# A linear-attention block with a gated MLP: two PSUM banks, two engines' copies, one early load and a new issue order

## The chip, the cores and the metric

The kernel runs on one core of a Trainium2 chip. The metric is the device time of one execution in microseconds, as a median over several executions. A profile is one further execution with the hardware profiler on; its span is some 2 us shorter than the timed figure, so spans are compared with spans and medians with medians. All profiled runs here ran at a granted TensorE clock of 1.0 and are of state fast.

## The reference, cut to what matters

The input x has 2048 tokens of 512 features, all in bf16. The attention is linear: phi(q) and phi(k) in place of a softmax, 32 heads of 16 features.

```python
phi = lambda t: jnp.where(t > 0, t + 1, jnp.exp(t)) + 1e-06
pq, pk = (phi(q), phi(k))
kv  = jnp.einsum('bhsd,bhse->bhde', pk, v)
z   = jnp.einsum('bhsd->bhd', pk)
num = jnp.einsum('bhqd,bhde->bhqe', pq, kv)
den = jnp.einsum('bhqd,bhd->bhq', pq, z)[..., None] + 1e-06
o   = num / den
...
h  = x + o @ wo                               # after a layer norm of x in front
z  = gelu(layernorm(h) @ w_in)                # 2 x 896 features
z1, z2 = z[..., :896], layernorm(z[..., 896:])
g  = jnp.einsum('ts,bsf->btf', w_sp, z2) + b_sp[None, :, None]
h2 = h + (z1 * g) @ w_out
```

In the kernel, z1 is called the ungated half, z2 the gated half. The kernel folds kv and wo into one 512 x 512 matrix m, so that h is one product of pqT (phi of q, divided by the denominators) with m, plus x.

## The kernel before

The program first lists its operations, each with the tiles that it reads and writes, and from these works out every dependence. Then an issue order, a stored list of 1011 operation numbers, fixes in which order each engine issues its own. An operation waits by semaphore for what it depends on, so the order changes waits and never results. The parts that matter:

```python
ORDER = "c-jrogMtt..."                      # cut: 1011 operation numbers, packed
...
load_x("SP", 0, 1, 2150)                    # x0: one tile of 128 tokens, 128 KB
load_x("ACT", 1, 1, 2300)
x2 = load_x("SP", 2, 1, 2300)
load_x("ACT", 3, 1, 2550)
first_load("SP", wqkv[:, 0:2, D:2 * D], ..., "wka", 4200)       # K weights, 256 KB each
wk = first_load("ACT", wqkv[:, 2:4, D:2 * D], ..., "wkb", 4400)
for n, lat, behind in ((4, 3000, x2), (6, 3200, x2), (8, 3850, wk), ...):
    load_x("SP", n, 2, lat, behind)         # two tiles, 256 KB, held until `behind` has landed
```

```python
for c in range(KD):                          # m = kvm . wo, four column blocks
    b = CB[1 - c % 2]
    matmuls(bank(b), [(kvm[:, c, :], wo[:, c, :])])
    act(m[:, c, :], bank(b), ACT.Copy, GW)
```

The ungated half is made of six tile columns by Strassen's scheme, in cells of seven products of two matmuls each (0.43 us), and of a seventh column by plain, "classical", products of four matmuls (0.86 us). A cell owns the four banks 4 to 7, in one of two rotations. What counts is what must happen between the products of one cell:

```python
def strassen(k, q, banks, p5):
    A, B, C, E = banks
    ...
    matmuls(quad(A), list(zip(w11, a11)))
    copy(bank(B), bank(A))                                  # ScalarE
    matmuls(quad(E), list(zip(t1, s1)))
    copy(p5, bank(E))                                       # ScalarE
    matmuls(quad(A), list(zip(w21, a12)), **onto)
    gelu(k, q, 0, A)
    matmuls(quad(B), list(zip(t2, s2)), **onto)             # needs the first copy
    dve(... bank(C) = bank(B) + p5 ...)                     # line 856, VectorE
    matmuls(quad(B), list(zip(t3, s3)), **onto)             # writes the bank that line 856 reads
    ...
for q in (0, 1):
    for tg in (2 * q, 2 * q + 1):
        classic(KF - 1, tg, 6)                              # seventh column, bank 6
    ...
    for k in range(HF):
        strassen(k, q, ZB[cells % len(ZB)], p5z[cells % 2])
```

Because the classical products of the second half of the tokens use bank 6, and come first in program order, they must be done, GELU included, before a Strassen cell of that half writes bank 6.

The first products of the gates (each eight matmuls, 1.73 us) and the products of the gated half (also eight, in bank pairs 0/1 and 2/3) are independent of the cells. I call such a group a filler: it keeps TensorE streaming while another engine reads a bank.

Of the kernel before, what the change touches and what calls it, by code (L numbers as in the profile page):

```python
# [8 lines left out]
ACT = mybir.ActivationFunctionType  # L9
ALU = mybir.AluOpType  # L10

P = 128
# [3 lines left out]
ORDER = "c-jrogMttU00qE@tj)G<d$VoZwz=81ZQHhO+jiZ}FHA&4MpVQ_03sm@q9HnBASPlVHsT;Y5+E1yAUE;?AdJumgRlsO;0S?m2#=5uk{}V1A{mk+1yUju5+fh-BNYmu5YnPNDxw0Kpb{D(9uguo(x4y;BONlJ2+|`EnUE1hQ4Cp88C8%OjnNcYP!-uw1KCj=-BAKv(F5I364j6c)zJ*i(Go4t6TQ#}z0n3WQ46h53bj!Obx|5+Fb3mL5A`t?<FO1&upDjC8aYuG<<K7O&>sWP7yZxy4bTvSFc3@85uI=t2XO?4FaZ-W8I!OAE3q0=Fb#vT4na7IV~BuNIDz9Bg5el}kywLK7>%izj?U<U8JLOrSb&o_jagWT^;nBDIE5E@iOG73DVnP1c!t@SgP|CP4cLf9Sd2~Bf$f-!dDx6C*o!^biGA3G-8hG{*otj9kNr4+E4YelxPaukh!jexRJx8ExP+Uyj9Yk%*LZ_hxQ#owi~G2T2MErG2*HqihX{Ox07m3{JjN4*W>|({DE`DJe83NU#AkfLH^kt-|GR(TJHFx%Vlo!PGaP>-G9xi6qi~wyG7e)i9#b(IQ!_L3Fh8>}I`c9O$*eRBFdqvtEz>bQGcY5?zX--mEXA^{$%M?t?99QOEX`a@z;cYwKo(+Q7GY7=VKLTXU6$YyCSqciXBpP!V%B2|wq^xZWF=N+71n11He@3<W^N{7awcVQCS!NDWG}8^8&+ixR%Z(KW;3Q_6Sm?~F5_CZWlwJ5R+eOHZDShs;ZP3a6pr9jj^uRC;Bby&HP&ELHfMTeP&>9~U+!UMrBzn#Wfo;uPMu*oWm5-sWIuLdS7uUwX4G~L;AoEFSPo<^1u?hssWS(09LIA9cXB4DaTaHDIp=UL=kYAh@jTaY0w?hT^XLe3sDJ{MSA~>cg;iWdRZvBAhwHh4CA5(jSxP0<jnmbIGc<$~IiLGjM!UG1`+0yzSxm=xmz7jnl~qnxc$}Mfj|+K_D|mt{d6I*<fQvYpr+A4oHA}NKM{|`-^E6)zv`~vwR^@e-Z&*QZSy4}TjaBrN&sbH}^oRHPjt^K}?^#0+d7Xb*Tc=r9{|G(j3*O)(zT{0d)nhi+WxnET-r{E7CiQ_e^@Yt<OJDhobrfFTxrz}KponUsAN<LW{Kfiepcbm9;0mFTil_K$rr$io!%U#n3?<3>#Lx<(u!^SWilKyxsYFVwBx<NeYOS_vshw)2U23CtilktQtoHiMSW2o+imfP$qi~9<xZ0?#I<L;^pdRX~ZtAED>aL#ZqCM)PUh1oU8mMjRuT8q7!RoC68ls^Zra>C6AdS)p?bB&J)M%a2SdGzmZP5;$)plLc1dY@<P0~88)_QH$8g0;8?bjn+)NUQrL><*$9nxhT&@mm?RUOuK9nn*r&~2U5HGS7f-O(vM(Oo^$3%%AGJr{gKFZDw=^;oZTPm8rgOSMePwL&YkN^kW}A9YK$d|warUVrsdAM{0E^+})gOW*Wce^kY^9L#n~|5H5&cL;ZIeTQ@?hjBQEc0&g^g2OtzQ#+EYx|$<9s-ro&J359_Ii{<-iPN~YV>_1PxRc{Mq2s!<<2i{FyM_}uk<&VzlRKHyJEJqWsq470Gdq(TIE$M(tFt?&v$>UPI*)U^ky|^5bGe`cozHEY--TSnh270{-POfh)XiPoJzUCVT*4*Y$E97?E!@)O+{JBO(cN9%ecjHL+|TXZ)6+f3z1-WAJ;hT!%`-gHgFVZ$-QNQ|$8$Zz^SsdWy};|e!Hd1fOT5ur9pvF2=*>Rv6CUAB9_lUL=3yS`?cV7Ze(6yj>m45Lah~Au9^;9g<Xzt5WnSUkUgNbs<&!?`Gd}BA-sipE@1?%z<v!r^KIhk7<&{3_BR=GVzTn5c<jcO|Cw}Uye&%bw;ak4r>%QsRe&`3j=evIEcYf~=PT>Ns?1;|mbx!IEj^Z~y=EHvO)qdpr{^<VzBaZh("  # L16
# [236 lines left out]
def bass_sequential_preLN__linear_attn_block__mixer_gmlp__prompt_kernel(  # L253
# [241 lines left out]
    for n, lat, behind in ((4, 3000, x2), (6, 3200, x2), (8, 3850, wk), (10, 4000, wk), (12, 4200, wk), (14, 4400, wk)):  # L495
        load_x("SP", n, 2, lat, behind)
# [234 lines left out]
    for c in range(KD):  # L731
        b = CB[1 - c % 2]
        matmuls(bank(b), [(kvm[:, c, :], wo[:, c, :])])
        act(m[:, c, :], bank(b), ACT.Copy, GW)
# [5 lines left out]
    DB, MERGE = 6, ()  # L740
# [7 lines left out]
    for tg in range(NG):  # L748
# [12 lines left out]
        if tg not in MERGE:  # L761
# [3 lines left out]
            for t in range(first, tg + 1):  # L765
                for c in range(0, KD, 2):
                    q, r = pqT[:, c:c + 2, t * GW:(t + 1) * GW], r16[t // 2][:, c:c + 2, t % 2, :]
                    dve(lambda v, q=q, r=r: v.tensor_tensor(q, q, r, ALU.mult), [q, r], [q], 2 * GW, acc=2)
# [116 lines left out]
    cells = 0  # L885
    for q in (0, 1):
        a11, a12, a21, a22 = (hx[:, 2 * i:2 * i + 2, 4 * q:4 * q + 4, odd, :] for odd in (0, 1) for i in (0, 1))
        for tg in (2 * q, 2 * q + 1):
            classic(KF - 1, tg, 6)
            for fc in CLASSIC.get(tg, ()):  # L890
                classic(fc, tg, 6)
# [193 lines left out]
```

## Time and profile before

| | before |
|---|---|
| time, median of 3 runs | 230.85 us (230.7 to 230.99) |
| profiled span | 229.2 us |
| TensorE busy | 221.9 us, 97% |
| VectorE, ScalarE, GpSimd busy | 174.5, 109.6, 47.7 us |

The view that the argument rests on most is the chain of work that ended last, in order of time: start, length, engine, output tile, line. Wherever it leaves PE, TensorE waited. One place of it that the prediction does not show is between two products of the gated half (L807 and L810), right after ScalarE has loaded its GELU table:

```profile
69.30 0.86 PE psum L807 x4
70.16 0.65 PE psum L810 x4
70.81 0.02 issue
70.83 1.04 PE psum L807 x4
```

Two such products stand back to back, and the second takes 1.04 us where its like takes 0.86: it waits for ScalarE to empty a bank.

For small stalls I use the starts of the matmul records: the step from one start to the next, less the step that this width has in packed stretches (0.216 us for 512 columns). I call the sum over a stretch its lost time. Matmuls that start together (the four of a group of denominators, within 0.01 us of each other) count as no loss and no gain. In the first traces of before and after one record in 49 is missing (1168 of 1191 are there), and the doubled steps at those places (shown as 0.05 us "issue") are left out. Steps from one kind of matmul to another have fixed costs of up to 0.1 us that all kernels share.

### The profile page before, as it was taken

The page shows a single profiled execution, that of the slowest core. Times are in us where ns is not written, and L with a number is a line of the kernel's source. Part 1 is how long each engine was busy: PE and PEld are TensorE (multiplying, and loading weights), DVE is VectorE, ACT ScalarE, POOL GpSimd, SP SyncE. Part 2 cuts the span into 40 slices and gives each one's busy share as a digit, 9 for nine tenths or more (in the row PEclk, how much of TensorE's full clock was granted, in tenths as well). Part 3 has the DMA queues.
Part 4 walks back from the last instruction along what each step waited for, and adds up shares of the span by engine and source line. Part 5 has one row for each costly group of instructions (what it writes and reads, how often), then busy time and mean ns, then how long its engine had stood idle before and what let it go on. Part 6 is the DMA issues. An engine that isn't in the chain of part 4 may idle for free.

```text
span 229.2 us, 3241 instructions
## 1 busy us (share of the span) xinstructions
PE 221.9 (97%) x1168; PEld 110.0 (48%) x1191; DVE 174.5 (76%) x347; ACT 109.6 (48%) x205; POOL 47.7 (21%) x134
## 2 busy tenths in 40 slices
PE   8899999999899999999999999999999999999995
PEld 7344444453344444444434444444455555555553
DVE  3999756937996979489988888678738688885295
ACT  5695943499889989999456102100022122021110
POOL 3444400000764584467600000000000000000000
PEclk9999999999999999999999999999999999999999
DMA  6942469928645149499900799800000000020025
GB/s 186 280 131 47 93 177 331 268 79 196 147 108 106 38 92 111 96 184 224 125 0 1 153 234 177 172 0 0 3 0 0 0 26 24 0 69 3 0 83 169
DMA packets 58896, 23.68 MB, mean 103 GB/s; under 512 B 48512, under 2 KB 58752, under 8 KB 58880
## 3 DMA queue, kind: packets, MB, share of 16 engines
q1 hardware_dynamic: 58176, 22.88, 44.8%
q10 hardware_dynamic: 704, 0.59, 0.8%
q8 instruction: 9, 0.15, 0.2%
q14 instruction: 7, 0.06, 0.1%
HBM read 7.47 MB, written 2.10 MB: 42 GB/s over the span
## 4 chain that ended last, share of the span: by engine, by line
PE 91%; DVE 2%; issue 2%; POOL 1%; DMA 1%; ACT 1%
PE psum L402 72%; PE psum L807 6%; PE psum L659 6%; PE psum L810 5%; DMA x<-in_A_x_dram 1%; ACT sh L421 1%; DVE h L981 1%; DVE h L781 1%; POOL rs L550 1%; ACT m L421 0%; PE psum L755 0%; POOL st L534 0%; PE psum L680 0%; PE psum L569 0%; PE psum L724 0%
## 5 line engine op out<-in xcount | busy, mean ns | idle before, releaser
L421 ACT ACTIVATE psum<-psum 128x256 f32<-128x256 f32 (+1 forms) x39 | 17.7, 467 | 83.6 <-PE psum L402 57.0
L402 PE MATMUL psum<-wsp,z 128*128 128x512 bf16 x200 | 47.6, 379 | 0.4
L402 PEld LDWEIGHTS psum<-wsp,z 128*128 128x128 bf16 x208 | 20.4, 98 | 22.5 <-ACT psum L421 0.2
L421 ACT ACTIVATE e<-psum 128x1024 bf16<-128x1024 f32 (+1 forms) x18 | 16.7, 927 | 12.7 <-PE psum L402 12.0
L402 PE MATMUL psum<-t,s 128*128 128x512 bf16 x96 | 22.5, 379 | 0.0
L421 ACT ACTIVATE z1T<-psum 128x512 bf16<-128x512 f32 x28 | 16.1, 601 | 8.1 <-PE psum L402 5.5
L402 PE MATMUL psum<-wsp 128*128 128x256 bf16 (+1 forms) x89 | 19.3, 315 | 0.4 <-DVE psum L856 0.4
L402 PE MATMUL psum<-wout,z1T 128*128 128x256 bf16 (+1 forms) x82 | 16.5, 314 | 0.1
L807 PE MATMUL psum<-win,hnT 128*128 128x512 bf16 x63 | 16.2, 379 | 0.1
L989 DVE TENSOR_TENSOR u<-psum,bsp 128x512 bf16<-128x512 f32 x16 | 11.0, 689 | 6.0 <-PE psum L402 5.9
L402 PE MATMUL psum<-xnT,wqkv 128*128 128x512 bf16 x61 | 15.2, 379 | 0.2
L659 PE MATMUL psum<-pk,xn 128*128 128x512 bf16 x64 | 15.3, 379 | 0.0
L421 ACT ACTIVATE z<-psum 128x896 bf16<-128x896 f32 x16 | 14.6, 913 | 1.3 <-PE psum L810 1.0
L402 PE MATMUL psum<-wqkv,xnT 128*128 128x512 bf16 x61 | 14.7, 379 | 0.2
L402 PE MATMUL psum<-m,pqT 128*128 128x512 bf16 x62 | 14.4, 379 | 0.3 <-DVE h L781 0.2
L989 DVE TENSOR_TENSOR u<-psum,p 128x512 bf16<-128x512 f32 x12 | 8.3, 688 | 8.1 <-PE psum L402 8.0
L402 PEld LDWEIGHTS psum<-t,s 128*128 128x128 bf16 x96 | 9.4, 98 | 10.0
L810 PE MATMUL psum<-win,hnT 128*128 128x384 bf16 x64 | 13.0, 326 | 0.0
L510 DVE BATCH_NORM_STATS2 st<-x 128x6 f32<-128x512 bf16 x15 | 9.7, 677 | 3.8 <-DMA x<-in_A_x_dram 3.8
L781 DVE SCALAR_TENSOR_TENSOR h<-psum,x 128x512 bf16<-128x512 f32 x16 | 10.8, 686 | 2.1 <-PE psum L402 2.1
L534 POOL TENSOR_SCALAR st<-st 128x1 f32<-128x1 f32 x10 | 3.9, 391 | 40.0 <-ACT sh L421 32.2
L402 PEld LDWEIGHTS psum<-wsp 128*128 128x128 bf16 x90 | 8.2, 98 | 8.2 <-DVE psum L856 1.0
(125 smaller groups left out, 382.4 us busy)
## 6 DMA issues: line engine op xcount, KB each, us to landing
r<-rcp SPq DMA_DIRECT2D x16, 128.0 KB, 2.7
out_dram<-h SPq DMA_DIRECT2D x15, 128.0 KB, 1.7
win<-in_B_w_in_dram SPq DMA_DIRECT2D x2, 896.0 KB, 5.5
x<-in_A_x_dram SPq DMA_DIRECT2D x6, 256.0 KB, 4.2
wqkv<-in_A_wqkv_dram SPq DMA_DIRECT2D x2, 512.0 KB, 5.8
wout<-in_B_w_out_dram SPq DMA_DIRECT2D x1, 896.0 KB, 7.3
wo<-in_A_wo_dram SPq DMA_DIRECT2D x1, 512.0 KB, 6.7
bsp<-in_B_b_sp_dram SPq DMA_DIRECT2D x1, 512.0 KB, 4.9
```

Source lines behind the costliest of these rows:

```text
L402: inst = pe.matmul(out_ap, lhsT=a, rhs=b, start=start and i == 0, stop=stop and i == len(pairs) - 1, **kw)
L421: return g.add("ACT", lambda ac: ac.activation(out_ap, in_ap, func, **kw), [in_ap, *extra], [out_ap] + ([accum] if accum is not None else []),
L510: dve(lambda v: v.bn_stats(s[:, 0:6], src[:, n, :]), [src[:, n, :]], [s[:, 0:6]], D)
L534: pool(lambda p: p.tensor_scalar(s[:, 2:3], s[:, 0:1], s[:, 0:1], -1.0 / (n * n), op0=ALU.mult, op1=ALU.mult), [s[:, 0:1]], [s[:, 2:3]], 240)
L550: pool(lambda p: p.tensor_tensor(r, ve, expo[:, 0:1], ALU.pow), [ve, expo], [r], 620)
L659: inst = pe.matmul(bank(CB[c]), lhsT=xn[:, i, c * P:(c + 1) * P], rhs=pk[:, i, :], start=i == 0, stop=i == NT - 1)
L781: dve(lambda v, n=n, b=b, s=s: v.scalar_tensor_tensor(h[:, n, :], bank(b), 1.0, x[:, n, :], op0=ALU.mult, op1=ALU.add, accum_out=s[:, 0:1] ...
L807: pe.matmul(bank(b), lhsT=hnT[:, c, n * P:(n + 1) * P], rhs=win2[:, c, 0:GW], start=c == 0, stop=c == KD - 1)
L810: inst = pe.matmul(bank(b + 1, F2), lhsT=hnT[:, c, n * P:(n + 1) * P], rhs=win2[:, c, GW:FH], start=c == 0, stop=c == KD - 1)
L981: dve(lambda v, o=o, q=q, add=add: v.tensor_tensor(o, q, add, ALU.add), [q, add], [o], DH2, ps=True)
L989: dve(lambda v: v.tensor_tensor(t, bank(b), add, ALU.add), [bank(b), add], [t], GW, ps=True)
```

## The change

The intent: give the last classical products banks that the pairs of the gated half have left, so that their place is less bound; halve ScalarE's copies of m; have x4 and x5 at hand earlier. The issue order was made anew for this.

```diff
-ORDER = "c-jrogMttU00qE@tj)G<d$VoZwz=81ZQ..."      (cut)
+ORDER = "c-jTQ17HvU00h8Cwq47%ZQHhO+qGre..."        (cut)
@@
-    for n, lat, behind in ((4, 3000, x2), (6, 3200, x2), (8, 3850, wk), ...
+    for n, lat, behind in ((4, 4600, None), (6, 3400, x2), (8, 3850, wk), ...
@@
         matmuls(bank(b), [(kvm[:, c, :], wo[:, c, :])])
-        act(m[:, c, :], bank(b), ACT.Copy, GW)
+        if c % 2:
+            dve(lambda v, c=c, b=b: v.tensor_copy(m[:, c, :], bank(b)), [bank(b)], [m[:, c, :]], GW, ps=True)
+        else:
+            act(m[:, c, :], bank(b), ACT.Copy, GW)
@@
+    last = [next_pair() + i for i in (0, 1)]           # banks 0 and 3
     for q in (0, 1):
         for tg in (2 * q, 2 * q + 1):
-            classic(KF - 1, tg, 6)
+            classic(KF - 1, tg, last[tg - 2] if q else 6)
```

The rest of the diff is a switch (PM) that would put products of pqT on GpSimd. It is empty in the change, so it does nothing there.

More of the change, by code (lines that the diff above doesn't have):

```diff
@@ L15 @@
 SEM_NS = 45.0
-ORDER = "c-jrogMttU00qE@tj)G<d$VoZwz=81ZQHhO+jiZ}FHA&4MpVQ_03sm@q9HnBASPlVHsT;Y5+E1yAUE;?AdJumgRlsO;0S?m2#=5uk{}V1A{mk+1yUju5+fh-BNYmu5YnPNDxw0Kpb{D(9uguo(x4y;BONlJ2+|`EnUE1hQ4Cp88C8%OjnNcYP!-uw1KCj=-BAKv(F5I364j6c)zJ*i(Go4t6TQ#}z0n3WQ46h53bj!Obx|5+Fb3mL5A`t?<FO1&upDjC8aYuG<<K7O&>sWP7yZxy4bTvSFc3@85uI=t2XO?4FaZ-W8I!OAE3q0=Fb#vT4na7IV~BuNIDz9Bg5el}kywLK7>%izj?U<U8JLOrSb&o_jagWT^;nBDIE5E@iOG73DVnP1c!t@SgP|CP4cLf9Sd2~Bf$f-!dDx6C*o!^biGA3G-8hG{*otj9kNr4+E4YelxPaukh!jexRJx8ExP+Uyj9Yk%*LZ_hxQ#owi~G2T2MErG2*HqihX{Ox07m3{JjN4*W>|({DE`DJe83NU#AkfLH^kt-|GR(TJHFx%Vlo!PGaP>-G9xi6qi~wyG7e)i9#b(IQ!_L3Fh8>}I`c9O$*eRBFdqvtEz>bQGcY5?zX--mEXA^{$%M?t?99QOEX`a@z;cYwKo(+Q7GY7=VKLTXU6$YyCSqciXBpP!V%B2|wq^xZWF=N+71n11He@3<W^N{7awcVQCS!NDWG}8^8&+ixR%Z(KW;3Q_6Sm?~F5_CZWlwJ5R+eOHZDShs;ZP3a6pr9jj^uRC;Bby&HP&ELHfMTeP&>9~U+!UMrBzn#Wfo;uPMu*oWm5-sWIuLdS7uUwX4G~L;AoEFSPo<^1u?hssWS(09LIA9cXB4DaTaHDIp=UL=kYAh@jTaY0w?hT^XLe3sDJ{MSA~>cg;iWdRZvBAhwHh4CA5(jSxP0<jnmbIGc<$~IiLGjM!UG1`+0yzSxm=xmz7jnl~qnxc$}Mfj|+K_D|mt{d6I*<fQvYpr+A4oHA}NKM{|`-^E6)zv`~vwR^@e-Z&*QZSy4}TjaBrN&sbH}^oRHPjt^K}?^#0+d7Xb*Tc=r9{|G(j3*O)(zT{0d)nhi+WxnET-r{E7CiQ_e^@Yt<OJDhobrfFTxrz}KponUsAN<LW{Kfiepcbm9;0mFTil_K$rr$io!%U#n3?<3>#Lx<(u!^SWilKyxsYFVwBx<NeYOS_vshw)2U23CtilktQtoHiMSW2o+imfP$qi~9<xZ0?#I<L;^pdRX~ZtAED>aL#ZqCM)PUh1oU8mMjRuT8q7!RoC68ls^Zra>C6AdS)p?bB&J)M%a2SdGzmZP5;$)plLc1dY@<P0~88)_QH$8g0;8?bjn+)NUQrL><*$9nxhT&@mm?RUOuK9nn*r&~2U5HGS7f-O(vM(Oo^$3%%AGJr{gKFZDw=^;oZTPm8rgOSMePwL&YkN^kW}A9YK$d|warUVrsdAM{0E^+})gOW*Wce^kY^9L#n~|5H5&cL;ZIeTQ@?hjBQEc0&g^g2OtzQ#+EYx|$<9s-ro&J359_Ii{<-iPN~YV>_1PxRc{Mq2s!<<2i{FyM_}uk<&VzlRKHyJEJqWsq470Gdq(TIE$M(tFt?&v$>UPI*)U^ky|^5bGe`cozHEY--TSnh270{-POfh)XiPoJzUCVT*4*Y$E97?E!@)O+{JBO(cN9%ecjHL+|TXZ)6+f3z1-WAJ;hT!%`-gHgFVZ$-QNQ|$8$Zz^SsdWy};|e!Hd1fOT5ur9pvF2=*>Rv6CUAB9_lUL=3yS`?cV7Ze(6yj>m45Lah~Au9^;9g<Xzt5WnSUkUgNbs<&!?`Gd}BA-sipE@1?%z<v!r^KIhk7<&{3_BR=GVzTn5c<jcO|Cw}Uye&%bw;ak4r>%QsRe&`3j=evIEcYf~=PT>Ns?1;|mbx!IEj^Z~y=EHvO)qdpr{^<VzBaZh("
@@ new lines @@
+ORDER = "c-jTQ17HvU00h8Cwq47%ZQHhO+qGrewr$(CZ5wxy5Czc?4-pX=Q4t+65EHQw8*z{Txe$On$c?;6f}{Y5a0rjk2m>Q5gkT7T2ndM~2##b(juc3VL`aNO$cOwWi~>lD3aEsNXo|{cjQB{1)JTIOD2Q~(fTBo`Ldb-SD2C$5iYlmz%xHpU$bxFfhMLHZ66k@F=!tIVj#8+O9H@a>sDtKcftF~6Ug(X!=!4d%jkYL_x~PXSD1)-7k8x;#u~>%jIE;f>jw3jPHfV>q$cb_&kM`(*0T_sW=#P%*gw9xkrI>(;n1rL4jAJ-~6<CSYScT)5f`({>!5D;*2*fl@#dHk8X#`;?hG7lXVH8HA3%X(kW@0`TU=~hdA<kee*5eeO<0W2TvYuj!o?$lTU^qr#12$q27Go23U_0hw9yVhO_F@lqVjp&4H_qZ5wqhI3V?Pey3a;WBF5n`r;|4C_CNAR^UgHg3;Vo|CF7DwD?&AT1^Bo={1Vi!>BJe#v;WIwq2fpDa9^(l@F)YI{G`}M}BQg>{;tRgw7yck7!GDOw*bK+t_={9b&8UpVD2&WJ%*_0Z!RXAw0!%|QE6I3_!?=vkv`okJ%)pGy%hD9fupslXEVD5?b1)|hu`r9UD2uTc%dswlu{?7zfC-q8nK)Isxr8lQn{8N}^;nY0)rxJ|gFTsuiCKY3n3N^BhP_#b^|_c!xr}Ssnx&YG$yt$=SeaGWfK}O$jo6q?Sc558jVaWesnnDy)rTp$g{ifNTiK3j)Qf$&m%}-NHQ9pI*`6KPk^R`8oj8D<*^E;d$n=`ZAdciVPUCcD)fvuUHxA?=4rUi-P)6<JC}z`Wj^RvZR$66II%QW*<<MEq;yRAya*pF{&f#2c=MK)}3XbPW9$_wJQf}o@KAqzP?&nZW;sGAydd_E8cIPxr<a7<=LQduoF5*!xU^30nOwH14&Cy)V(|j$^LM_rA=2Za|QehQQeic&*U13ob)G-#<U6xd7RaPl&U|GH4RbFFxz2$kn<9puYP9En8p5!i`;zk}~6CGwbRnQZbQ598GB|YUIR@WE)<uiWeH-=YmMNkM`;6FB14PE4OzThS9=4C?n`G60(iI4c5t5{VvRZCPIZDun?)CWe=YQE$vUgr(o<SqVSWJOU_N!CyP;zveTJyla}wNOjdReiNmYqe8I#ZY{;S99HF2X$5g1t_K-GnQg2m`*dHUh_9UF_c29joPY#x~QXis++p2lX|F;daJK?s-b$Rs~W4H`fGsVD6SGIng;1J2Wp7=D2&1?v63j9;_1AGX}B(EutsR4hH94rHA+dfQI|AYV>DLdwN;z6M-wzoleA8!wM}PqMf<c`o3&jJwL|N*Mr*ZS8+1{-bx>z@PJ4A!hqOfp^hk&GTu*dNM|4@obye4NLMQc9*Y!+6nyA})p&NRv@4BPAdaYA>qno;=#ag1JTBhY%p_N*tmx5pEp5E%6KI*<6=)FGahd$`1zUZ@R_?N!woBryz{wSqsIhgHK{-^p5?hx+i1`g>^4(%`w=SHsW2#)B~uIW0C=I9RV@UG>^j^Y@O=~%AnIF9XVuIK7*;<%3I_)g%2PU5Cc>}F2mhHmZvCvsY+b7v=WCntAfr*{TtbX{k5CTDSLXLnZTbT+qfZg+Jaw{;8Wa4r{gA?J5K7j{t>aTm9Aceipe7k4+8aA}uyNtbd@w{sbnb9;Ai4_9zy_jP&qbAR`8Z};(JPjMwr_h8TP5YO~%&+-5d^dL|3aZmMJ&+#zN^Fpupd~fgqZ}bR{^d@iiR&ViQFY*#^^G@&fcJFYIhkBRyc$CL_xJNtC<2>GDe8LmF)O)?p%e>zcJ;^71$_IVgXMENNyuvU1(yx5c%YEMGe8Go&#IJqSE4|jMyvC3H#Fu>8Pkq(bebcvn#n*hpw|vLXe9w3Nzz_Y_@BH2$oYW~?z<C|XQC-Cqeb~qR#_Rmt_r2PW{L%jbNviim"
@@ L494, in bass_sequential_preLN__linear_attn_block__mixer_gmlp__prompt_kernel @@
     wk = first_load("ACT", wqkv[:, 2:4, D:2 * D], A_wqkv[2 * P:4 * P, D:2 * D], "wkb", 4400)
-    for n, lat, behind in ((4, 3000, x2), (6, 3200, x2), (8, 3850, wk), (10, 4000, wk), (12, 4200, wk), (14, 4400, wk)):
+    for n, lat, behind in ((4, 4600, None), (6, 3400, x2), (8, 3850, wk), (10, 4000, wk), (12, 4200, wk), (14, 4400, wk)):
         load_x("SP", n, 2, lat, behind)
@@ L733, in bass_sequential_preLN__linear_attn_block__mixer_gmlp__prompt_kernel @@
         matmuls(bank(b), [(kvm[:, c, :], wo[:, c, :])])
-        act(m[:, c, :], bank(b), ACT.Copy, GW)
+        if c % 2:
+            dve(lambda v, c=c, b=b: v.tensor_copy(m[:, c, :], bank(b)), [bank(b)], [m[:, c, :]], GW, ps=True)
+        else:
+            act(m[:, c, :], bank(b), ACT.Copy, GW)
     while qs:
         q_unit(*qs.pop(0))
-    DB, MERGE = 6, ()
+    DB, MERGE, PM = 6, (), ()
     def spread(tg, c, w):
@@ L767, in bass_sequential_preLN__linear_attn_block__mixer_gmlp__prompt_kernel @@
                     q, r = pqT[:, c:c + 2, t * GW:(t + 1) * GW], r16[t // 2][:, c:c + 2, t % 2, :]
-                    dve(lambda v, q=q, r=r: v.tensor_tensor(q, q, r, ALU.mult), [q, r], [q], 2 * GW, acc=2)
+                    if (t, c) in PM:
+                        pool(lambda v, q=q, r=r: v.tensor_tensor(q, q, r, ALU.mult), [q, r], [q], 1800)
+                    else:
+                        dve(lambda v, q=q, r=r: v.tensor_tensor(q, q, r, ALU.mult), [q, r], [q], 2 * GW, acc=2)
     AB, HPAIR = [4, 5, 7], 2
```

## The prediction

> **What bounds the kernel now.** I read four views in this order: the page's busy shares, the chain of work that ended last, the list of waits of TensorE, and the timeline around each place where the chain leaves TensorE. The page says that TensorE is the bound:
>
> ```profile
> span 229.2 us, 3241 instructions
> PE 221.9 (97%) x1168; PEld 110.0 (48%) x1191; DVE 174.5 (76%) x347; ACT 109.6 (48%) x205; POOL 47.7 (21%) x134
> PE 91%; DVE 2%; issue 2%; POOL 1%; DMA 1%; ACT 1%
> ```
>
> Busy is not the same as streaming at full rate, so I checked the spacing. Eight 512-column matmuls in one line of the timeline take 1.89 us; one record lasts 379 ns, so their starts lie (1.89 - 0.379) / 7 = 0.216 us apart. That spacing holds nearly everywhere between 8.5 us and the end. The table of stretches gives 215.35 us busy of the 218.0 us between 8 and 226 us: 2.65 us idle. About 20 of those gaps are 0.05 us "issue" gaps, one every 49 matmuls, with exactly two spacings between the neighbours: a record is missing there, not time. That leaves some 1.6 us of real idle time. In that stretch the waits view gives TensorE's matmuls only three waits worth a line:
>
> ```profile
> PE psum L755 <- DVE pqT L584: 0.5, 1, 0.5
> PE psum L402 <- DVE psum L856: 0.4, 1, 0.4
> PE psum L402 <- DVE h L781: 0.2, 1, 0.2
> ```
>
> The chain in order of time says where they lie, and adds the start of the kernel, where TensorE waits for the second token tile:
>
> ```profile
> 6.69 0.24 POOL st L537
> 6.93 0.07 issue
> 7.00 0.58 POOL rs L550
> 7.58 0.03 issue
> 7.61 0.42 DVE xn L555
> 8.03 0.05 issue
> 8.08 0.40 PE psum L569 x4
> ...
> 52.23 1.09 ACT m L421 x2
> 53.32 0.05 issue
> 53.37 0.39 PE psum L402
> ...
> 61.17 0.74 DVE pqT L584 x2
> 61.92 0.46 issue
> 62.38 0.70 DVE h L781 x2
> ...
> 117.69 0.71 DVE psum L856
> 118.41 0.05 issue
> 118.45 0.60 PE psum L402 x2
> ```
>
> The first column is the start, the second the length. Each departure from PE is a place where another engine was late. The rest is packed, and the change removes no matmul: it can only win back such gaps.
>
> **What the Trainium skill says.** "Perfetto Trace Analysis", Identifying the Most-Contended Engine, warns that matmul busy share is no measure of headroom because matmuls are pipelined; I agree with it in using the spacing, and the spacing here says that there is nearly no headroom. "VectorE: DVE Perf Modes", section "Why PSUM operands drop a tier", says that a fp32 PSUM operand leaves VectorE at one element per cycle. The trace agrees: the mask product kvm, 512 fp32 elements out of PSUM, takes 0.69 us, the additions into h 686 ns. "ScalarE: Activation LUTs", What ACT_TABLE_LOAD costs, gives 186 ns + 0.833 ns per element, 613 ns for 512; the four copies of m measure 592 to 632 ns, median 608. So the copies get no cheaper on VectorE, they only run in another queue. "DMA: Bandwidth & Descriptors", "Issuing engines are not separate DMA queues", says that all loads share the same 16 engines; here those moved 331 to 335 GB/s from 3 to 5 us, so an earlier x4 load competes with the other first loads.
>
> **The change part by part.** The diff also replaces the issue order. I decoded both lists: the same 1011 operations, in many places in another order on every engine. So there are four parts.
>
> 1. *Head.* x4 and x5 (256 KB) no longer wait for x2. Before, their load was issued at 4.36 us and landed at 7.86, and their statistics began on VectorE at 7.93, right behind the normalization of x1 that TensorE waited for. They now go out at about 2.2, behind the first half of the K weights in the same queue, so they cannot delay x0 to x3 (landed 3.8 to 4.6); the weights (landed 5.9 and 6.1) are needed only at 8.5. By itself this saves nothing. But the new order also puts the square of x1 ahead of x0's logarithm on ScalarE. In the chain that logarithm (0.29 long, about 0.2 after overlap) lies between the two ScalarE sums of x1. So x1's transposes start about 0.2 us earlier, at 7.9, and VectorE, which is busy 7.78 of the 8 us from 8 to 16, can keep this lead only because x4 is already there. Gain: **0.2 us**.
> 2. *m copies.* Before, four ScalarE copies of 608 ns; now two. VectorE takes 2 x 0.69 = 1.38 us. It was idle 2.57 us before kvm and 1.41 us before the first product with r, so much of this lies in idle time. The kvm product moves ahead of a group of four q matmuls (0.86 us) but that group's exp, phi and pqT then move back by 0.86 us. I followed both queues by hand with the durations above: TensorE reaches the last h-independent group within 0.2 us of the old time. The waits on m themselves cost little (a missing record hides in the gap at 53.37: 0.10 idle where 0.05 is the missing record). Gain: **0**, give or take 0.2.
> 3. *Last two classical products.* Tile column 6 for token groups 2 and 3 goes to banks 0 and 3, which the ungated half's pairs have left, instead of sharing bank 6 with the Strassen cells. The matmuls stay (8 x 0.216 us); what goes is a write-after-read dependence on bank 6, and that lets the order change. At 118 us the old order has t2 product, one 0.43 us group, t3 product into the same bank. Between them VectorE must read the bank: 0.17 us until the result is visible, 0.70 for the addition, 0.05 for the semaphore, 0.92 in all; 0.43 is covered, 0.5 is not. The new order has a gating group of eight matmuls (1.73 us) there. Every other such pair that I looked at in the new order has 0.85 us or more between. Gain: **0.5 us**.
> 4. *The middle, 56 to 66 us.* Before, TensorE loses about 0.6 + 0.3 us at 62.5 and 63.1 (0.55 and 0.21 idle, the rest hidden in the modelled ends). VectorE sets this stretch: 9.21 of 10 us busy. The new order asks it for one more h group before the denominators and one m copy (0.69). TensorE gets one more h group (0.86) to run first. By hand: denominators and the eighth h group done by about 64.2, old 64.0. The four sums of the weight quarters (about 0.5 each) also move from 43 us into the stretch 66 to 80, where VectorE was busy 13.6 of 16 us (64 to 80). Gain: **0**, from -0.5 to +0.5.
>
> Sum: 0.2 + 0 + 0.5 + 0 = 0.7 us. The tail stays: the last store goes out some 0.4 us after the last matmul, and lands 2 us later. 230.85 - 0.7 = 230.15; I say **230.1 us**.
>
> **Rivals.** *A, VectorE becomes the bound from 50 to 80 us.* For: 92% busy from 56 to 66, and the change puts 1.4 us of copies and 2 us of sums nearer to it. Against: it still waited 0.58 and 1.26 us between 71 and 75 us, and 1.41 at 54. It would cost up to 1 us and give 231. *B, the order recovers the middle as well as 118 us.* For: eight h groups stand ahead of the denominators, not seven. Against: h evacuation on three banks holds TensorE to VectorE's pace. It would give 229.2. *C, the early x4 load delays x0 to x3 or the weights.* For: DMA engines 99% busy from 3 to 5 us. Against: it is issued after them, in the same queue as half of them, and the weights have over 2 us of slack. If x3 came late by the 0.8 us that 256 KB takes at 331 GB/s, the time would be up to 0.8 us longer: 231.
>
> **Range and chances.** Everything that can be won is the head's fraction of a microsecond and 1.6 us of gaps, so under 227.5 or so is out of reach; faster by over 2% means under 226.2. Slower by over 2% means 4.6 us of new stalls, over twice all the old ones; a reordering could make one, but each reordered group has other matmuls to cover it. Range **229.1 to 231.3**: B's 229.2 near the low end, A and C together near the upper. Chances: faster 0.01, within 2% 0.97, slower 0.02.
>
> **What would show it.** Head: x1's transposes at about 7.9 us, not 8.08; x4 landing about 6.5 to 7. Part 2: two m copies on VectorE at about 0.69 us each. Part 3: no wait of TensorE on L856 (its line moves a little) near 118 us. Part 4: the wait of L755 on pqT smaller or gone, but waits on h in its place, summing to 0.5 to 1 us between 56 and 66. TensorE's busy time should stay within 1 us of 221.9. The prediction is wrong if TensorE shows a gap over 1 us anywhere after 9 us, if the head moves later, or if the end moves in a stretch where I expect none, such as 120 to 226 us, which I hold to be packed in both.

## The result, and the profile after

The kernel after takes 230.07 us (median of 6 runs, 229.56 to 230.45); before, in the same rounds, 230.95 (6 runs, 230.7 to 231.2). The ratio is 0.9959, 95% interval 0.9946 to 0.9973: 0.4% faster, clearly below 1. Here and below a ratio is the mean time of one kernel's fast runs over that of the other's of the same rounds, so it is not quite the ratio of the medians quoted beside it.

The page of the kernel after, its span, busy shares and chain by engine:

```profile
span 228.4 us, 3248 instructions
PE 221.9 (97%) x1168; PEld 110.1 (48%) x1191; DVE 174.5 (76%) x349; ACT 108.5 (48%) x203; POOL 47.1 (21%) x134
PE 87%; DMA 4%; DVE 3%; ACT 3%; issue 1%; POOL 1%; SPq 1%; DVEq 0%
```

TensorE has the same work, to the tenth of a microsecond. Its share of the chain fell from 91% to 87%, which by itself is no loss: the head and the middle now lead back through a DMA instead of through GpSimd and ScalarE. The waits of TensorE's matmuls between 8 and 226 us (total, times, longest):

```profile
PE psum L813 <- DMA hnT<-hn: 0.3, 1, 0.3
PE psum L569 <- DVE xn L555: 0.3, 1, 0.3
PE psum L402 <- DVE h L787: 0.2, 1, 0.2
PE psum L724 <- ACT ct L421: 0.2, 1, 0.2
```

The two largest waits of before, on pqT and on the Strassen addition (L856, now L862), are gone; two new ones stand at the top, one at the first gated product (64.16 us), one at x4's transposes (11.79 us). At 118 us, where before lost half a microsecond, the chain after stays on PE, with only a missing record:

```profile
107.54 10.36 PE psum L402 x48
117.90 0.05 issue
117.95 10.74 PE psum L402 x49
```

And the gated products after the table load (L813, L816) no longer stand back to back; a group of four matmuls for h lies between, and nothing is stretched:

```profile
69.30 0.65 PE psum L816 x4
69.95 0.86 PE psum L402 x4
70.81 0.86 PE psum L813 x4
```

Following the same work in both traces tells where the time went (of the K product, the record of the very first matmul is missing in both, 0.22 us earlier: 8.31 and 7.92 us):

| position | before, us | after, us | after less before |
|---|---|---|---|
| first recorded matmul of the K product | 8.53 | 8.13 | -0.40 |
| x4's transposes | 11.83 | 11.79 | -0.04 |
| third denominators | 53.69 | 53.74 | +0.05 |
| first gated product | 64.00 | 64.16 | +0.16 |
| last matmul | 226.32 | 225.50 | -0.81 |

So the head gains 0.40 us and loses 0.36 of it within 4 us. From there to the first gated product the kernel after loses another 0.2. Everything that stays comes after 64 us: 0.97 us. By lost time, 0.35 of it is in 66 to 108 us, 0.54 in 108 to 121, and 0.09 in the last 10 us of matmuls (221.97 us).

### The profile page after: what moved, and what is told of

Its sections match the earlier page's. It is cut to its first block, busy times and chain, and to the rows that moved or that the text cites. A ratio compares the mean times of both kernels' runs of the same rounds, so it can differ in the third digit from the quotient of the medians.

```text
span 228.4 us, 3248 instructions
## 1 busy us (share of the span) xinstructions
PE 221.9 (97%) x1168; PEld 110.1 (48%) x1191; DVE 174.5 (76%) x349; ACT 108.5 (48%) x203; POOL 47.1 (21%) x134
## 4 chain that ended last, share of the span: by engine, by line
PE 87%; DMA 4%; DVE 3%; ACT 3%; issue 1%; POOL 1%; SPq 1%; DVEq 0%
PE psum L402 69%; PE psum L659 6%; PE psum L813 6%; PE psum L816 4%; DMA x<-in_A_x_dram 2%; DMA hnT<-hn 1%; DVE st L510 1%; ACT ct L421 1%; SPq L432 1%; ACT pqT L421 0%; PE psum L724 0%; PE psum L680 0%; ACT z L421 0%; DVE h L988 0%; ACT sh L421 0%
## 5 line engine op out<-in xcount | busy, mean ns | idle before, releaser
L402 PE MATMUL psum<-wsp,z 128*128 128x512 bf16 x201 | 47.8, 379 | 0.4
L402 PEld LDWEIGHTS psum<-wsp,z 128*128 128x128 bf16 x208 | 20.3, 98 | 23.0
L402 PE MATMUL psum<-t,s 128*128 128x512 bf16 x95 | 22.3, 379 | 0.1
L402 PE MATMUL psum<-wsp 128*128 128x256 bf16 (+1 forms) x87 | 18.9, 313 | 0.2
L813 PE MATMUL psum<-win,hnT 128*128 128x512 bf16 x63 | 16.4, 379 | 0.3 <-DMA hnT<-hn 0.3
L402 PE MATMUL psum<-wout,z1T 128*128 128x256 bf16 (+1 forms) x81 | 16.2, 313 | 0.0
L402 PE MATMUL psum<-xnT,wqkv 128*128 128x512 bf16 x61 | 15.1, 379 | 0.2
L402 PE MATMUL psum<-m,pqT 128*128 128x512 bf16 x62 | 14.6, 380 | 0.4 <-DVE h L787 0.2
L402 PE MATMUL psum<-wqkv,xnT 128*128 128x512 bf16 x61 | 14.7, 379 | 0.2
L402 PEld LDWEIGHTS psum<-t,s 128*128 128x128 bf16 x96 | 9.4, 98 | 10.0
L581 DVE TENSOR_SCALAR e<-e 128x1024 bf16<-128x1024 bf16 (+1 forms) x18 | 7.0, 391 | 8.1 <-ACT e L421 7.9
L816 PE MATMUL psum<-win,hnT 128*128 128x384 bf16 x64 | 13.0, 326 | 0.0
L510 DVE BATCH_NORM_STATS2 st<-x 128x6 f32<-128x512 bf16 x15 | 9.9, 674 | 3.8 <-DMA x<-in_A_x_dram 3.8
L402 PEld LDWEIGHTS psum<-wsp 128*128 128x128 bf16 x90 | 8.7, 98 | 6.8 <-DVE wsp L1001 0.4
```

What stands on the lines that cost most here:

```text
L402: inst = pe.matmul(out_ap, lhsT=a, rhs=b, start=start and i == 0, stop=stop and i == len(pairs) - 1, **kw)
L510: dve(lambda v: v.bn_stats(s[:, 0:6], src[:, n, :]), [src[:, n, :]], [s[:, 0:6]], D)
L581: dve(lambda v: v.tensor_scalar(e, e, 1.0, EPS_PHI, op0=ALU.min, op1=ALU.add), [e], [e], w * GW, acc=4)
L813: pe.matmul(bank(b), lhsT=hnT[:, c, n * P:(n + 1) * P], rhs=win2[:, c, 0:GW], start=c == 0, stop=c == KD - 1)
L816: inst = pe.matmul(bank(b + 1, F2), lhsT=hnT[:, c, n * P:(n + 1) * P], rhs=win2[:, c, GW:FH], start=c == 0, stop=c == KD - 1)
```

## The experiments

Twelve runs. Each has its lost time by stretch in this table; "-" means under 0.01 us.

| run | ratio to before, 95% interval | 56-66 | 66-108 | 108-121 | 121-160 |
|---|---|---|---|---|---|
| before | 1 | 1.12 | 0.35 | 0.54 | - |
| after | 0.9959 (0.9946 to 0.9973) | 1.23 | - | - | - |
| e1 x4 held | 0.9962 (0.9945 to 0.9979) | 1.07 | - | - | - |
| e2 x4 before weights | 0.9946 (0.993 to 0.9962) | 1.16 | - | - | - |
| e3 m all on ScalarE | 1.0036 (1.002 to 1.0051) | 0.90 | 0.56 | - | - |
| e4 gate group moved | 1.0009 (0.9993 to 1.0025) | 1.14 | 0.45 | 1.03 | - |
| e5 new front, old back | 1.0066 (1.0051 to 1.0082) | 1.40 | 1.80 | 0.54 | - |
| e6 old front, new back | 0.9954 (0.9939 to 0.9969) | 1.13 | 0.17 | - | - |
| e7 after, bank 6 | 1.0099 (1.008 to 1.0117) | 1.46 | 0.86 | 2.30 | - |
| e8 a product on GpSimd | 0.9996 (0.9982 to 1.0011) | 2.42 | - | - | - |
| e9 other filler moved | 1.0029 (1.0009 to 1.0049) | 1.13 | 0.45 | - | 1.71 |
| e10 pqT later | 0.9957 (0.994 to 0.9974) | 1.36 | - | - | - |
| e11 after again | 0.9957 (0.994 to 0.9975) | 1.08 | - | - | - |
| e12 e2 again | 0.994 (0.9927 to 0.9954) | 1.13 | - | - | - |

(Before has 0.35 in 66-108 with records missing; e4 and e9, which leave that stretch unchanged and have all records, have 0.45. In e3 the first gated product came so late, at 66.26 us, that its wait counts into the next stretch. e3 has 1.55 us of idle time at 55.4 and e9 is the only run with a loss after 121 us but for under 0.1 us in the tail. The text on record for e3 gives after 0.59 us in 56-66: it counted the four denominators that start together as 0.64 us gained. One wait stands in no column: at about 21 us TensorE loses 0.02 to 0.35 us in the ten traces with the new front and 0.00 in the four with the old one; in e1 and e2 it is a product of wqkv with xnT that waits for a transposing DMA.)

After the first look my theory was: the gain is order and banks behind 64 us; the hold of x4 and the copies of m are worth nothing. The rivals were the prediction's own head lead, and that the copies on VectorE carry something.

### e1: the hold put back

```diff
-    for n, lat, behind in ((4, 4600, None), ...
+    for n, lat, behind in ((4, 4600, x2), ...
```

> The kernel after with one part undone: the load of x4 and x5 waits again for x2 to have landed, as it did before. Theory (from the two traces: x4 and x5 landed at 7.86 us in both kernels, held or not, and without the hold the first two loads of K weights landed 1.1 us later, at 7.0 and 7.2 instead of 5.9 and 6.1): the hold is worth nothing to x4. With it back, x4 lands between 7.6 and 8.1, the weights land at about 6.0, the stall of TensorE before x4's transposes near 11.8 us keeps its 0.4 us, and the time is that of the kernel after, 230.1, within 0.15 us. Rival (the prediction on record): the unheld load feeds VectorE and keeps a head lead of 0.2 to 0.4 us; with the hold back the time is 230.3 to 230.5 and the first K matmul or x4's transposes come 0.2 us or more later than in the kernel after.

Measured: 230.47 us, ratio 0.9962; after has 0.9959 and 0.9957. By the letter the rival was met: the median lies in its 230.3 to 230.5, and x4's transposes came at 12.06, 0.27 us later than in after. But before was 0.17 us slower in these rounds too, and the interval of the ratio is 0.4 us to either side, so the time decides nothing on 0.2 us; the landings must. The chain of this run shows what sets x4's transposes (L569), from the load through the statistics (L510):

```profile
4.23 3.91 DMA x<-in_A_x_dram
...
8.16 1.29 DVE st L510 x2
...
12.06 0.41 PE psum L569 x4
```

In the kernel after, the same chain begins at 2.18 us and is no shorter:

```profile
2.18 5.68 DMA x<-in_A_x_dram
...
7.88 1.29 DVE st L510 x2
...
11.74 0.05 issue
11.79 0.40 PE psum L569 x4
```

Every further run gave one more sample of the head, so the question could be settled over ten traces. The loads of the head land at slightly different times from one execution to the next:

| us | x4 held (before, e1, e4, e6, e9) | x4 not held (after, e3, e5, e7, e11) |
|---|---|---|
| x4 issued | 4.06 to 4.36 | 2.18 to 2.19 |
| x4 landed | 7.18 to 8.13, mean 7.81 | 7.56 to 8.29, mean 7.87 |
| later half of the K weights landed | 6.12 to 6.85, mean 6.55 | 6.95 to 7.75, mean 7.28 |

Issued 2 us earlier, x4 lands at the same time. What the earlier issue does is to delay the weights, by 0.7 us, which nobody notices because they are wanted only at about 8. In eight of these ten traces x4's transposes start 3.92 or 3.93 us after x4's landing, whatever happened ahead of it. In before the step is 3.97 and in e9, where x4 landed at 7.18, 4.44; there the order of TensorE's own work ruled, some 3.5 us after its first K matmul. In e1 my number for the landing, 7.6 to 8.1, just missed 8.13, the weights came at 6.48 and 6.65 and not at about 6.0, and the wait was 0.6 and not 0.4 us.

### e2 and e12: x4 ahead of the weights

```diff
+    load_x("SP", 4, 2, 4600, None)
     first_load("SP", wqkv[:, 0:2, D:2 * D], ..., "wka", 4200)
...
-    for n, lat, behind in ((4, 4600, None), (6, 3400, x2), ...
+    for n, lat, behind in ((6, 3400, x2), ...
```

The stored order has the three loads' numbers exchanged to match.

> The kernel after with the load of x4 and x5 put ahead of the first load of K weights in SyncE's queue, unheld. Theory (x4 lands late because it shares the transfer with two 256 KB loads of weights that were given out ahead of it; the weights are needed only at 8.1 us): x4 lands at 5.5 to 7.0 instead of 7.86, the weights at 7.0 to 7.5, and the 0.4 us stall of TensorE near 11.8 us shrinks to under 0.15; x0 to x3 land within 0.15 us of where they were, and the time goes down by 0.2 to 0.4, to 229.7 to 229.9. Rival one: order within one queue decides little, the transfers share the engines evenly, and x4 lands again after 7.5: no change, 230.1. Rival two: VectorE works through its statistics in order and not x4's landing but that chain sets the 11.8 us: x4 lands earlier and the stall stays, 230.1.

> The second run's kernel again (the kernel after with x4 and x5 loaded ahead of the K weights), to see whether its lead over the kernel after repeats. Theory (x4's transposes start at the later of two times: 3.93 us after x4 has landed, or about 3.5 us after the first K matmul; with x4 at 7.0 us the first no longer binds): x4 lands at 6.9 to 7.2 us, TensorE does not wait at 11.4 to 11.6 us, and the ratio to before is 0.993 to 0.9955, median 229.7 to 229.95. Rival (the first measurement was a lucky sample and the gain of up to 0.4 us is eaten later, where the first gated group waits for the normalised h): ratio 0.9955 to 0.997.

Measured in e2: x4 landed at 7.03 us (a little over the upper end of what I expected), the weights at 7.46 and 7.93 (the second later than expected), and TensorE's wait near 11.8 is gone: the transposes start at 11.47. Time 229.85 us, ratio 0.9946. In e12: 229.79 us, ratio 0.994. Its profile missed my numbers in the head: x4 landed at 7.48 and the second half of the weights at 8.24, so that now TensorE waited for the weights, 0.2 us before its first K matmul at 8.33 (0.39 by the steps), while x4's transposes (11.78) no longer waited. So here the place in the queue decided who came first, and the wait moved from x4 to the weights. It became smaller on average: between 8 and 13 us TensorE lost 0.0 to 0.4 us in the four traces with x4 ahead (e2, e8, e10, e12; mean 0.16), and 0.1 to 0.9 in the six with the new order and x4 behind (after, e1, e3, e5, e7, e11; mean 0.49). After and after again have 0.9959 and 0.9957, so the two means differ by 0.0015 of 231, an estimate of 0.35 us; the intervals still overlap. This version had the lowest ratios of all that ran. It is faster than before for certain; that it is faster than after is likely and not shown: the profiled spans, 228.1 and 228.5, are no shorter than after's 228.4 and 228.1, and e10, which has the same loads, has 0.9957.

### e3: all copies of m on ScalarE, in the new order

```diff
-        if c % 2:
+        if False:
             dve(... tensor_copy(m[:, c, :], bank(b)) ...)
```

> The kernel after with one part undone: all four copies of m on ScalarE again, at the same places of the order. Theory (the chain at 52 to 54 us ends in a copy on ScalarE in both kernels, and the stretch 56 to 66 is bound by VectorE, which is busy without a pause from 56.5 us on, but had idle time before 54): moving two copies of 0.69 us each off VectorE at 51.3 and 53.5 us makes nothing earlier there, ScalarE has 1.2 us more to do; the third wait for m near 53.4 grows from 0.19 to between 0.3 and 0.8 us, the PE waits after 56 us stay within 0.3 us, and the time is 230.1 to 230.6. Rival (VectorE is the bound of the middle and any copy taken from it helps): the excess of 0.59 us in TensorE's stretch 56 to 66 us falls by 0.3 or more and the time is 229.6 to 229.9.

Measured: 231.94 us, ratio 1.0036, far outside both expectations: 1.8 us worse than after by the ratios. The chain of this run:

```profile
53.62 0.59 ACT r L421
...
54.24 0.63 ACT rcp L421
54.87 0.50 ACT m L421
...
55.41 0.40 PE psum L402
```

TensorE waits 1.55 us for the copy that frees a bank for the third product of kvm and wo. On ScalarE that copy stands behind the logarithm and the exponential of the second denominators (r and rcp), which the new order put there because in it VectorE makes this copy meanwhile. So I had left the order out: a copy that changes its engine within a fixed order also changes its place. Whether ScalarE could do it in an order of its own is the next run's question.

### e5 and e6: halves of the two orders

e5 takes each engine's order from after up to the first gated product and from before behind it, with bank 6 for all classical products. e6 is the reverse: x4 held, all copies of m on ScalarE and before's order up to that point, after's order and banks behind it.

```diff
 e5: order = new[up to the first gated product] + rest in old order;  classic(KF - 1, tg, 6)
 e6: order = old[up to the first gated product] + rest in new order;  hold and m copies as before
```

> A kernel of two halves: every engine follows the order of the kernel after (x4 unheld, two copies of m on VectorE) up to the first group of the gated half, at about 64 us, and the order of the kernel before from there on, with all four last classical products in bank 6. Theory (the gain of 0.9 us lies wholly behind 64 us: in the two traces the first gated group starts at 64.00 us before and 64.16 us after): the time is that of before or a little over it, ratio 0.998 to 1.003; the waits of before at about 66.5 and 70.8 us (0.14 and 0.18 us) and the 0.5 us near 118 us are back, TensorE's excess is 0.2 to 0.4 us in 66 to 108 us and 0.45 to 0.6 us in 108 to 121 us. Rival (the prediction's head lead, or the m copies, carry part of it): ratio 0.996 to 0.998.

> The opposite halves: x4 held, all m copies on ScalarE and the order of the kernel before up to the first gated group at about 64 us, then the order of the kernel after, with the last two classical products in banks 0 and 3. Theory (the gain lies behind 64 us): the whole gain of the kernel after is there, ratio to before 0.994 to 0.997, with no stall of over 0.1 us near 118 us and TensorE's excess under 0.1 us in 66 to 121 us; the wait of 0.7 us near 62.5 us stays. This would also clear the run with all m copies on ScalarE, which lost 1.8 us to the kernel after: there ScalarE kept an order made for two copies on VectorE, and here it has its own order back, so that its wait for m near 53.4 us is 0.1 us and not 1.55. Rival (the m copies on VectorE are worth something by themselves): ratio 0.998 to 1.002, or a wait for m of over 0.5 us.

e6: 230.17 us, ratio 0.9954; after has 0.9959. With nothing of the new front, the whole gain is there. The waits of TensorE in e6: that on pqT is back, that on the Strassen addition is not.

```profile
PE psum L758 <- DVE pqT L584: 0.5, 1, 0.5
PE psum L569 <- DVE xn L555: 0.4, 2, 0.3
PE psum L402 <- DVE h L787: 0.2, 1, 0.2
```

ScalarE, in its own order, makes all four copies of m and TensorE waits 0.1 us for them. So the gain needs neither the copies on VectorE nor the unheld load; whatever they add is within the interval, 0.35 us to either side.

e5: 232.74 us, ratio 1.0066, worse than expected. The 0.54 us at 118 us (here at 120.7) and 0.18 us between the back-to-back gated products came back as expected, the 0.14 us near 66.5 did not, and where the two orders meet a new wait of 1.33 us appeared, at 68.72: the four sums of weights that the old order makes at about 43 us and the new one after 66 fell on one spot and held VectorE from 65.65 us for 2 us, ahead of two reads of h. This is an accident of the cut, so e5 carries little. Taking the 1.33 us off, an estimate, would leave about 231.4.

### e4 and e9: the order alone at 118 us

Both are the kernel before, bank 6 and all, with one gate group moved in TensorE's order. The names below: first, E, t2, A, t3 and C are products of one Strassen cell (t2 and t3 the pair that shares a bank), G1 and G2 two gate groups, N the first product of the next cell. G1, in bank 1, reads the second half of z2 (the text on record says the first).

```diff
 before:  E, first, G1, t2, A, t3, C, G2, N        (first: the cell's first product)
 e4:      E, first, t2, A, G1, t3, C, G2, N
 e9:      E, first, G1, t2, A, G2, t3, C, N
```

> The kernel before with one group of eight matmuls (the first of a gate's, bank 1, reads the first half of z2 and of the spatial weights) moved two groups later, so that it stands between the second and third product of one Strassen cell; nothing else, no bank changed. Theory (the 0.54 us stall at 118 us is TensorE waiting for VectorE to read the bank that it is about to write again; eight matmuls of 216 ns cover that read): the stall at 118 us is gone, TensorE's excess in 108 to 121 us falls from 0.54 us to under 0.05, and the time falls from 230.95 to 230.4 (230.2 to 230.55). Rival (the stall is closed by the free bank of the last classical products, so the order alone moves it to another place): the stall comes up again within 10 us, and the time stays at 230.8 to 231.1.

> The kernel before with the other gate group at hand (second half of z2, bank 3, which stood after the cell, just ahead of the next cell's first product in bank 7) moved up between the second and third product of the Strassen cell at 118 us; no bank changed. Theory (the second half has one filler group too few, wherever it is put): the 0.5 us at 118 us go, and the next cell's first product, which needs bank 7 back from a GELU that ended at 120.43 us in the kernel before, now stands at 119.3 to 119.5 us and waits there 0.8 to 1.2 us for ScalarE; the time is 231.1 to 231.7, ratio 1.001 to 1.003. Rival (an order alone, with the last classical products left in bank 6, closes the gap; the first swap merely took the wrong group): no wait of over 0.1 us between 116 and 122 us and ratio 0.997 to 0.9985.

e4: 231.42 us, ratio 1.0009. My theory fell here. The wait at 118.45 us is gone, but a larger one stands 2 us earlier:

```profile
115.71 0.58 ACT psum L421
...
116.34 1.68 PE psum L402 x7
```

TensorE (idle 0.86 us) waits for ScalarE's copy of the cell's first product, which the gate group had covered. It had not been idle cover that could be moved. The rival's "moves to another place" was right, though not its time (231.42 us for 230.8 to 231.1); that the lack is one of free groups was the new theory, which e7 and e9 then tested.

e9: 231.9 us, ratio 1.0029, which the theory formed from e4 had put at 1.001 to 1.003 (its time, 231.1 to 231.7, was too low). Nothing is lost at 118 us, and the next cell pays:

```profile
120.91 1.58 ACT z1T L421 x3
...
122.54 1.04 PE psum L402 x4
```

The next cell's first product waited 0.99 us for a GELU to free bank 7 and the one after it 0.37 us more for bank 6 (1.2 us and 0.5 us by the steps). So in the order of before the fillers are one too few for this stretch: at both places tried, closing the gap opened another.

### e7: the new order with bank 6

```diff
-            classic(KF - 1, tg, last[tg - 2] if q else 6)
+            classic(KF - 1, tg, 6)
```

> The kernel after with the last two classical products in bank 6 again, as before; the order is that of after but for what the bank forces: these two groups of four matmuls and their GELUs have to come before the Strassen products that use bank 6, so they no longer stand between the Strassen products of the second half. Theory (formed after the swap of one gate group in the kernel before only moved the stall from 118.45 to 116.34 us and from VectorE's read to ScalarE's copy: each Strassen cell needs two or three groups of other work between its own, and in the kernel before there was one too few; the free banks give two such groups back): stalls come back, 0.3 to 0.8 us between the two products, which follow each other in one bank, and 0.1 to 0.5 us in the cells that lost them, near 113 and 117 us; TensorE's excess in 100 to 121 us is 0.5 to 1.3 us and the time is 230.6 to 231.4. Rival (the bank is an accident and only the order of the gate groups matters): excess under 0.15 us and 230.1.

Measured: 233.43 us, ratio 1.0099, 3.2 us slower than after by the ratios; direction as the theory said, size above its range. The waits of TensorE in this run:

```profile
PE psum L402 <- ACT z1T L421: 1.4, 2, 0.7
PE psum L402 <- ACT psum L421: 0.7, 1, 0.7
PE psum L402 <- DVE psum L866: 0.4, 1, 0.4
```

The first line comes from the two classical products, forced to an earlier place and following each other in bank 6: the second waits 0.69 us for the GELU of the first, at 106.83, and the Strassen product that takes bank 6 next waits 0.69 us for the GELU of the second, at 108.56. The other two are a ScalarE copy (114.91 us) and a Strassen addition (112.33 us) that the classical products had covered in the new order. Not all of the 3 us is the bank's: with bank 6 a better order exists, namely that of before. What the run shows is that the new order lives on the two groups having free banks. The four runs together: order alone, in the two forms tried, gains nothing (e4, e9); the new order without the banks is worse (e7); both together gain the 0.54 us (after, e6). The fourth corner, the old order with the two free banks, was not run: there the same 0.43 us would stand between the same two products in bank 5, so I expect the wait to stay, but that is argued and not shown.

### e8: one product of pqT on GpSimd

On e2's kernel. VectorE is busy from 56.3 us on but for 0.3 us at 60.0, and TensorE waits for it twice, so I took a product away from it.

```diff
-    DB, MERGE, PM = 6, (), ()
+    DB, MERGE, PM = 6, (), ((1, 2),)
```

> The second run's kernel (x4 and x5 loaded ahead of the K weights, 229.85 us) with one of the two products of pqT with r of the second quarter of tokens on GpSimd instead of VectorE: VectorE had done it at 57.5 us for 0.69 us, GpSimd was idle until 58.4 us and r was stored and on its way from 52.7 us. Theory (VectorE runs without a pause from 56.3 us, and TensorE's waits at 59.46 and 61.40 us, 0.38 and 0.20 us, end in its reads of h): these two waits fall to under 0.1 us each, but the first gated group, which waits for the first tile of normalised h through ScalarE's square, GpSimd's four small steps and a DMA, does not come earlier than 63.7 us: its wait grows from 0.37 by as much as the two others shrink, and the time stays within 0.15 us of 229.85. Rival (VectorE is the bound of the stretch): the gated group starts 0.4 us or more earlier and the time is 229.3 to 229.5. Risk: GpSimd takes over 3 us for it and delays h, 230.3 or more.

Measured: 231.06 us, ratio 0.9996: 1.2 us lost, in the expected stretch but for a reason that I had not named. GpSimd took 2.12 us, less than my risk of 3. These two lines of the timeline (start, length, engine, line) tell the rest:

```profile
55.91 2.12 POOL L773 TENSOR_TENSOR pqT<-pqT,r 128x1024 bf16<-128x1024 bf16 x1 [30.87 <-DMA r<-rcp]
56.16 2.42 DVE L585 TENSOR_TENSOR pqT<-pqT,e 128x1024 bf16<-128x1024 bf16 x1 [0.65 <-ACT pqT L421]
```

VectorE's product of two SBUF tiles, 0.69 us in e2, took 2.42: it ended 0.55 us after GpSimd's, as if it had begun only then. The first read of h came 1.6 us later than in e2. The Trainium skill says this on the page "SBUF — State Buffer", section "Who interferes with whom": a VectorE instruction with two SBUF inputs contends with a GpSimd instruction that reads SBUF, and the port pair that they share is an exclusive lock. The trace agrees, with 2.42 us against 0.69. Whether a VectorE relieved of this product would have started the gated products earlier is therefore not answered.

### e10: a VectorE operation put later

On e2's kernel, in VectorE's order only: the combination of pqT with e for the last quarter (0.69 us) moved from ahead of the first read of h to behind the fifth.

```diff
 VectorE: -pqT(254), h0, pqT.r, pqT.r, h1, h3, hn0, h2, e, h4, pqT(260), h5
          +h0, pqT.r, pqT.r, h1, h3, hn0, h2, h4, pqT(254), e, pqT(260), h5
```

> The second run's kernel (x4 and x5 loaded ahead of the K weights) with one operation of VectorE put later: the combination of pqT with its exponential for the last quarter's first half, 0.69 us at 56.3 us, stood ahead of the first read of h, though its result is wanted only by the last denominators at 63.3 us; it now stands after the read of the fifth h, and that fifth h ahead of the next step of e. No engine, bank or load changed. Theory (the first gated group waits through a chain that begins at the first read of h: square on ScalarE, four small steps on GpSimd, normalisation, DMA; that read waits only for VectorE): the first read of h starts 0.2 to 0.3 us earlier, at 56.6, and the first gated group as much earlier; the waits at 59.46 and 61.40 us (0.38 and 0.20) fall by 0.2 or more in sum, and the time is 0.2 to 0.3 us under that of the second run: ratio to before 0.993 to 0.9945. Rival (the normalised h comes by DMA at its own time, or the last denominators now wait): the gated group starts within 0.1 us of 63.91 us and the ratio stays 0.9945 to 0.996.

Measured: 230.02 us, ratio 0.9957: the rival was right. The first read of h did start at 56.62 (56.90 in e2), the wait for the fourth bank of h fell from 0.38 to 0.18 us, and then the last denominators waited 0.38 us for pqT, where e2 did not wait. The first gated product started at 63.89 (63.91). The transposing DMA went out 0.26 us earlier and brought its tile no earlier. What bounds this stretch from that side stays open.

### e11: the kernel after again

> The kernel after, unchanged, on the same chip as the two other runs, to compare with them and to see how far its head moves from run to run: ratio to before 0.995 to 0.997, TensorE's excess under 0.05 us from 66 us on. x4 lands at 7.8 to 8.1 us and TensorE waits 0.2 to 0.7 us for it near 11.8 us; if it waits under 0.1 us, the wait at the head is chance and not the loads' order.

Measured: 230.02 us, ratio 0.9957. x4 landed at 7.60, below my 7.8 to 8.1, and TensorE lost only 0.10 us at x4's transposes (11.53), where I had expected 0.2 to 0.7. The profiled span was 228.1, against 228.4 for the same kernel before: 0.3 us, of which 0.26 is there at x4's transposes already, so it comes from the landing of the first loads. A single profile of this head is not worth more than that.

## Why the prediction was right, and where it was not

The time was right: 230.1 predicted, 230.07 measured. The sum was 0.7 us and the medians differ by 0.88. But the sum's terms were not all right; two errors of opposite sign met, and that the total came so close is luck.

1. **Head, "0.2 us": failed.** Half of its mechanism holds. The new order on ScalarE does start x1's transposes earlier: 3.94 to 4.0 us after x1's landing in all traces with the new head, 4.04 to 4.09 in those with the old one, so 0.1 us. Most of the 0.4 us that the two first profiles show is x1 landing 0.27 us earlier, by chance. The step that failed is "VectorE ... can keep this lead only because x4 is already there", with "x4 landing about 6.5 to 7": x4 landed at 7.86, as before, and VectorE waited for it. I had read off that the load is issued earlier and that the engines are busy at that time, and not drawn the conclusion that both together mean a landing at the same time. Issue is not landing; ten traces give 7.81 us held and 7.87 not held. Rival C, that the early load delays the weights, came true to 0.7 us on average and cost nothing, as I had argued from the slack, though not for the reason given ("same queue").

2. **Copies of m, "0, give or take 0.2": right.** The two on VectorE took 0.69 and 0.68 us. e6 shows the whole gain without them. e3 shows that this holds only for each order with its own engine: the same copies on ScalarE at the new places cost 1.8 us.

3. **The gap at 118 us, "0.5 us": right.** It was 0.54, no wait on that line is left, and none of the other pairs waits. That dropping the dependence on bank 6 "lets the order change" is what e7, e4 and e9 bear out. ("The ungated half's pairs" is a slip: the pairs of banks belong to the gated half.) What my text did not see is why a filler is free there: not the eight matmuls of the gate, which before were needed elsewhere, but the classical products, which now cover ScalarE's copy in their stead.

4. **The middle, "0": right in size, in part by luck.** The wait on pqT is gone and waits on h stand in its place, 0.38 and 0.19 us. The first gated product was put at 64.2 and came at 64.16, but not for the reason given: TensorE had done the denominators and the eighth h group by 63.72, and then lost 0.44 us waiting for the DMA that brings the first normalised h, which I had not listed. It took 3.17 us from issue to landing (60.94 to 64.11), before 2.41 (60.95 to 63.36); why it is longer stays open. By steps, the stretch 56 to 66 lost 1.12 us before and 1.23 after.

5. **What the sum left out.** The text expected nothing behind 66 us but the one gap. It found 0.35 us in 66 to 108 us and 0.09 in the tail. About half of the first is the pair of gated products back to back: 0.18 us in before and e5, none in after and e6, so it belongs to the new order behind 64 us. I had the chain with its 1.04 us (70.83) in front of me and looked only at waits of 0.2 us and more. The 0.14 us at 66.53 goes with the front (e6 still has 0.155), and the front that avoids it comes 0.16 us later, so little is left of it.

So the mechanism of the gain was right, rival A (VectorE as the bound, 231) did not come, and rival B (the middle recovered as well) did not either. TensorE's busy time stayed at 221.9, no gap exceeded 1 us, and 120 us to the tail was packed in both.

## What to carry to other kernels

Where the bound engine is 97% busy, as here, independent groups of work may be a stock that is already spent: here moving one closed one gap and opened another, twice, and only a change that made two groups movable (a bank that is free at the time) added to the stock. An earlier issue of a load need not be an earlier landing: x4, issued 2 us earlier behind the same transfers, landed no earlier. Change its place in the queue, and look at what then comes later. And an engine change for an operation is hard to judge at a fixed order, since the order was made for the engine: the copies of m cost 1.8 us on ScalarE in one order (e3) and nothing measurable in the other (e6).

## What the Trainium skill lacked or had wrong

- "DMA: Bandwidth & Descriptors": it says that all loads interleave on the same 16 engines, with which the traces fit, but gives no measured landings for a load issued early. Here 256 KB issued at 2.18 us landed at 7.87 on average and issued at 4.06 to 4.36 us at 7.81, while two loads of 256 KB ahead of it landed 0.7 us later; put ahead of one of these it landed at 6.97 to 7.48 (e2, e8, e10, e12).
- The same page has no figure for how far one and the same first load moves from run to run: x0, issued at 0.79 to 0.80 us in every trace, landed between 3.40 and 3.81.
- "PSUM — Partial Sum Buffer": no figure for how long a bank is lost to TensorE when another engine must read it between two products. Here a VectorE addition of 512 fp32 elements takes 0.70 us, and with two matmuls in between TensorE still stood idle for 0.36 us (before, 118.45 us); a GELU between two products of one bank left it idle for 0.69 us with nothing in between (e7).
- "GPSIMD Engine Reference", section "Elementwise — side-by-side cycle accounting", compares tensor_tensor on fp32 alone (1.96 times VectorE's time). For 128 x 1024 in bf16 it took 2.12 us here, against 0.69 on VectorE, 3.1 times (e8).
- "Perfetto Trace Analysis" says nothing of missing matmul records; in the two first profiles 23 of 1191 are missing, one in 49, and most show as an idle gap of 0.05 us (L402 at 117.90 us in after).
- Nothing that the skill states was found wrong; its statement on VectorE and GpSimd blocking each other held (e8: 2.42 us instead of 0.69).
